# Causal attention and a cosine MLP in one kernel: GpSimd's copy of q and k moved ahead of the halves of x

## The chip, the cores and the metric

The kernel runs on one core of one Trainium2 chip. The metric is the device time of one execution in microseconds. Times of the trace are counted from the start of its span. PE is the matrix engine, PEld its weight load, DVE is VectorE, ACT is ScalarE, POOL is GpSimd, and SP issues most of the DMAs.

## The reference

```python
# q, k, v: 4 batches, 12 heads, 448 positions, 64 per head, float32
scores = scale * q @ k^T                      # causal: masked above the diagonal
attn   = softmax(scores)
x      = (attn @ v) as [4*448, 12*64]         # 1792 x 768
h      = x @ w_in                             # 768 x 2048
out    = (h * cos(h)) @ w_out                 # 2048 x 768
```

All is float32. The kernel keeps that precision in the matrix products of the second part by splitting a number into a high half and a low half and multiplying three pairs of halves.

## The kernel before

The schedule is written out by hand: each engine takes its instructions in the order in which the program lists them, and an instruction that must wait holds up all that stand behind it on its engine or queue.

Attention is a loop over 24 pairs of heads (steps i = 0 to 23). Each step works on several pairs at once: the scores, masks and exponentials of pair i; the product of the probabilities with v, and the division, of pair i-2; the transposes of the probabilities of pair i-1; and the transposes of q and k of pair i+2.

- q and k of a pair are loaded by SP into one of two buffers `raw` (`load_raw`, L260; one buffer lies in the tile `land`, the other is the tile `raw`). GpSimd copies them into one of two buffers `nat`, which both lie in `land`, with the two heads side by side (`interleave`, L267). PE transposes `nat` (`transpose_in`, L336), and the result is evacuated to `flat` (`evac_in`, L340 and L342). Pairs 0 and 1 are loaded straight into `nat`.
- The scores (L383) go to PSUM, and DVE adds the mask and takes the row's minimum in one instruction for each of seven parts (`masked`, L392). ACT takes the exponentials (`exps`, L399).
- The probabilities are transposed on PE (`tp`, L416) and evacuated to `pm` by DVE (L340) and ACT (L342). `av` multiplies them with v (L436), and DVE divides (`divide`, L464 to L466).
- `put_out` transposes the quotient on PE (L475), ACT copies it to `xf` (L494), and GpSimd makes the high half and the low half of x from it (`finish_hi`, L499 and L500), which go to `xa` and `xb`. In some steps x is cut between these two and the halves are four instructions.
- Beside this, the weights of the first groups are converted: SP loads a piece into `st` every second step (L117, L122), DVE works on it (L139 and L142 in one step, L148 and L152 in the next), and GpSimd does the rest (L145, or L156 and L157), which the program keeps in the list `postponed` and lists at the start of the next step (`take_postponed`).

Before the change a step begins on GpSimd's queue with the copy of pair i+2, then the postponed weight work, and near the step's end come the halves of x of pair i-2. On SP's queue a step begins with the load of pair i+3, then v of pair i. In steps 0, 1 and 2 the order is written out on its own.

After attention the second part follows, in which PE works on large products; the loads of its weights go through the tile `land` as well, once attention has done with it.

Of the kernel before, what the change touches and what calls it, by code (L numbers as in the profile page):

```python
# [21 lines left out]
def kernel(  # L22
# [205 lines left out]
    def attention(filler_of, postponed):  # L228
        with (
# [15 lines left out]
            N = len(pairs)  # L245
# [7 lines left out]
            def half(h):  # L253
                return slice(h * R, (h + 1) * R)

            def load_raw(i):
                b, hp = pairs[i]
                raw[i] = raw_t[i % 2]
                for h, src in ((1, k), (0, q)):
                    nc.sync.dma_start(  # L260
                        out=raw[i][half(h)],
                        in_=src[b, 2 * hp : 2 * hp + 2].rearrange("j (p c) d -> p j (c d)", c=NM),
                    )

            def interleave(i):
                nat[i] = nat_t[:, i % 2]
                nc.gpsimd.tensor_copy(  # L267
                    nat[i].rearrange("p c (j d) -> p c j d", j=2),
                    raw.pop(i).rearrange("p j (c d) -> p c j d", c=NM),
                )  # L270
# [60 lines left out]
            def transpose_in(i, bs, order=None):  # L331
                for h in range(2):
                    qkt[i, h] = flat[:, 2 * h + i % 2, 0:S], banks8[:, bs[h], 0:S]
                for c, h in order or [(c, h) for c in range(NM) for h in range(2)]:
                    o = qkt[i, h][1].rearrange("p (r c) -> p c r", c=NM)
                    nc.tensor.transpose(o[:, c], nat[i][half(h), c], ident[half(h), half(h)])  # L336
# [7 lines left out]
            def evac_in(i, h, dve=False):  # L344
                evac(*qkt[i, h], dve)
# [11 lines left out]
            def col(m):  # L357
                return slice(COL[m], COL[m] + 1)

            def open_step(i):  # L360
                prob[i] = prob_t[i % 3]
                stats[i] = at.tile([P, 8], F32, tag="stat", bufs=3, name="stat")
# [4 lines left out]
            def place(i, m):  # L367
                b, o = spot(i, m)
                return banks8[:, b, o * R : (o + m) * R]

            def probs(i, m):
                return prob[i][:, AT[m] * R : (AT[m] + m) * R]
# [16 lines left out]
            def masked(i, *ms):  # L389
                for m in ms:  # L390
                    z = W if m == TURNED else S - m * R
                    nc.vector.tensor_tensor_reduce(  # L392
                        out=probs(i, m), in0=place(i, m), in1=mask[:, z : z + m * R], scale=-scale,
                        scalar=3.0e38, op0=ALU.add, op1=ALU.min, accum_out=stats[i][:, col(m)],
                    )

            def exps(i, *ms):
                for m in ms:
                    nc.scalar.activation(  # L399
                        probs(i, m), probs(i, m), AF.Exp, scale=-1.0, bias=stats[i][:, col(m)]  # L400
                    )
# [66 lines left out]
            def turn_out(i):  # L468
                t = outs[i].rearrange("p b n d -> p b (n d)")
                for x in range(4):  # L470
                    for h, ms in enumerate((ROW[1::2], ROW[::2])):
                        if x < len(ms):
                            b, n, _ = PLACE[ms[x]]
                            c = (T0, 4 * R)[h] + x * R
                            nc.tensor.transpose(  # L475
                                banks8[:, obank(i) + 1 - h, c : c + R],
                                t[half(h), b, n * P : (n + 1) * P], ident[half(h), half(h)],
                            )
# [9 lines left out]
            def finish(i):  # L488
                xf = at.tile([P, S], F32, tag="xf", bufs=2, name="xf")
                x = xf.rearrange("p (n r) -> p n r", r=R)  # L490
                ob = obank(i)
                for e, (b, c) in ((1, (1, T0)), (0, (0, 4 * R))):
                    o = banks8[:, ob + b, c : c + (4 - e) * R]
                    nc.scalar.copy(x[:, e::2], o.rearrange("p (n r) -> p n r", r=R))  # L494
                return xf

            def finish_hi(i, xf):
                for hi, lo, cs in x_of(i):
                    nc.gpsimd.tensor_copy(hi, xf[:, cs])  # L499
                    nc.gpsimd.tensor_tensor(lo, xf[:, cs], f32(hi), op=ALU.subtract)  # L500
# [3 lines left out]
            def fill(n):  # L504
                if not extra:
                    spare = itertools.cycle((7, 6))
                    extra.append(filler_of(lambda: banks8[:, next(spare)]))
                for _ in zip(range(n), extra[0]):
                    pass
# [7 lines left out]
            def put_out(i):  # L517
                turn_out(i)
                finish_hi(i, finish(i))

            def take_postponed():
                while postponed:
                    postponed.pop(0)()
# [7 lines left out]
            interleave(2)  # L531
            load_v(0)
            for i in range(N):
                if 2 < i + 2 < N:
                    interleave(i + 2)
                take_postponed()
                if i + 3 < N:
                    load_raw(i + 3)
                if i:
                    load_v(i)  # L540
                open_step(i)
                if i < 3:
                    scores(i, slice(0, 4))
                    if i < 2:
                        transpose_in(i + 1, TB_)
                    else:
                        tp(0, 1, (0, 1))
                    scores(i, slice(4, 8))
                if i == 0:
                    masked(i, 4, 3)  # L550
                    exps(i, 4)
                    evac_in(1, 0, True)
                    evac_in(1, 1)
                    masked(i, 7, 6, 5, 1, 2)
                    exps(i, 3, 7, 6, 5, 1, 2)
                    yield i
                    continue
                if i == 1:
                    masked(i, 4, 3, 7)
                    evac_in(2, 0)  # L560
                    evac_in(2, 1)
                    exps(i, 4, 3)
                    open_ptr(0)
                    tp(0, 0, (0, 1))
                    evac_out(0, 0, (0, 1), 0)
                    masked(i, 6, 5, 1, 2)
                    exps(i, 7, 6)
                    yield i
                    continue
                if i == 2:  # L570
                    transpose_in(3, TB_)
                    evac_out(0, 1, (0, 1), 0)
                    exps(1, 5, 1, 2)
                    masked(i, 4, 3)
                    exps(i, 4, 3)
                    masked(i, 7, 6)
                    exps(i, 7)
                    evac_in(3, 0, True)
                    evac_in(3, 1)
                    masked(i, 5, 1, 2)  # L580
                    exps(i, 6, 5, 1, 2)
                    av(0)
                    divide(0)
                    transpose_in(4, TB_)
                else:
                    scores(i)
                    if i < N - 1:
                        evac_in(i + 1, 0)
                        evac_in(i + 1, 1)
                    masked(i, 4, 3, 7, 6, 5, 1, 2)  # L590
                    exps(i, 4, 3, 7, 6, 5, 1, 2)
                    av(i - 2)
                    divide(i - 2)
                    if i < N - 2:
                        transpose_in(i + 2, TB_)
                G1, G2 = ((7, 4), (5, 6)) if i < N - 1 else (TB_, (4, 5))
                open_ptr(i - 1)
                tp(i - 1, 0, G1)
                evac_out(i - 1, 0, G1, 0)
                tp(i - 1, 1, G2)  # L600
                evac_tp(i - 1, 1, G2, 1)
                evac_tp(i - 1, 1, G2, 0, i % 2 == 0)
                if i == N - 1:
                    fill(4)
                put_out(i - 2)
                if i == N - 1:
                    fill(2)
                    open_ptr(i)
                    tp(i, 1, (4, 5))
                    evac_out(i, 1, (4, 5), 0)  # L610
                    tp(i, 0, TB_)
                    evac_out(i, 0, TB_, 0)
                yield i
# [785 lines left out]
    with tc.manual_schedule():  # L1399
        def filler_of(get):  # L1400
            return m1(ring, 0, *order_a[0], early, get)
# [75 lines left out]
```

## Time and profile before

| | |
|---|---|
| median of 3 runs | 600.83 us |
| lowest and highest run | 599.5 and 601.18 us |
| time of the profiled execution | 601.19 us |
| its span | 599.4 us |
| PE busy | 581.5 us, 97% |
| PE weight loads busy | 538.8 us, 90% |
| DVE busy | 455.2 us, 76% |
| POOL busy | 417.7 us, 70% |
| ACT busy | 402.2 us, 67% |

The shares are averages over the whole span. The attention loop and the second part have different limits, so a change in one of them is read from the rows of that part. The span is shorter than the time of the execution by 1.8 us.

### The profile page before, as it was taken

Reading aid. Unit: us, or ns where it says so; the run is one execution under the profiler, and the core shown is the slowest. Engines: PE = TensorE matmul, PEld = TensorE weight load, DVE = VectorE, ACT = ScalarE, POOL = GpSimd, SP = SyncE. Lnnn points to the kernel's source line nnn. Section 1 sums busy time; section 2 is a strip of 40 time slices with the busy share of each in tenths; the row PEclk is TensorE's granted clock in tenths of the full one; section 3 lists DMA queues with packets and bytes.
Section 4 is the critical chain, followed back from the end, with each engine's and each line's share of the span. In section 5 each row is a group of like instructions: output and inputs, shape, how many; then the busy total and the mean of one; then the engine's idle time right before and its main releaser. Section 6 shows DMA issues by size and latency. Waiting matters only on the chain.

```text
span 599.4 us, 15299 instructions
## 1 busy us (share of the span) xinstructions
PE 581.5 (97%) x5895; PEld 538.8 (90%) x5895; DVE 455.2 (76%) x952; ACT 402.2 (67%) x788; POOL 417.7 (70%) x448
## 2 busy tenths in 40 slices
PE   8999998899999999999999999999999999999996
PEld 6788887788899998899999999999999999999996
DVE  4889888887586787787777777853487887887786
ACT  5999998888667786877777778731544653654540
POOL 1466565654559786878778887744579878878894
PEclk9999999999999999999999999999999999999998
DMA  9958778565058868787969788499988547648105
GB/s 171 202 142 187 174 178 196 129 167 160 10 189 273 329 194 323 240 309 241 348 196 335 249 270 322 173 338 390 394 294 308 209 149 275 220 170 297 52 1 158
DMA packets 92601, 134.30 MB, mean 224 GB/s; under 512 B 35024, under 2 KB 76864, under 8 KB 92528
## 3 DMA queue, kind: packets, MB, share of 16 engines
q1 hardware_dynamic: 84832, 106.91, 57.8%
q0 software_dynamic: 4928, 24.78, 11.3%
q10 hardware_dynamic: 2768, 1.64, 1.0%
q8 instruction: 46, 0.75, 0.5%
q14 instruction: 27, 0.22, 0.1%
HBM read 83.36 MB, written 49.94 MB: 222 GB/s over the span
## 4 chain that ended last, share of the span: by engine, by line
PE 73%; POOL 6%; ACT 6%; DVE 5%; DMA 5%; issue 3%; SPq 0%; ACTq 0%; POOLq 0%; DVEq 0%
PE banks L733 18%; PE banks L1162 13%; PE banks L1182 13%; PE banks L638 6%; PE banks L637 6%; PE banks L639 6%; POOL land L267 3%; ACT pm L342 2%; PE banks L336 2%; PE banks L1199 2%; PE banks L416 2%; PE banks L1086 2%; PE banks L436 2%; DMA vn<-in_v_dram 2%; DMA land<-in_moe_w_in_dram 2%
## 5 line engine op out<-in xcount | busy, mean ns | idle before, releaser
L721 DVE TENSOR_TENSOR acc<-acc,banks 128x768 f32<-128x768 f32 (+1 forms) x122 | 112.6, 932 | 42.3 <-PE banks L733 32.1
L733 PE MATMUL banks<-w,gh 128*128 128x384 f32 x512 | 109.9, 335 | 1.2 <-DVE acc L721 1.2
L733 PEld LDWEIGHTS banks<-w,gh 128*128 128x128 f32 x512 | 90.7, 188 | 3.0 <-DVE acc L721 1.8
L638 PE MATMUL banks<-xa,w 128*128 128x512 f32 x192 | 75.2, 392 | 0.0
L639 PE MATMUL banks<-xa,w 128*128 128x512 f32 x192 | 75.0, 391 | 0.0
L637 PE MATMUL banks<-xa,w 128*128 128x512 f32 x192 | 74.9, 390 | 0.0
L399 ACT ACTIVATE pb<-pb,stat 128x256 f32<-128x256 f32 (+6 forms) x168 | 71.1, 527 | 3.3 <-DVE stat L392 3.3
L392 DVE CUSTOM_DVE_ANT_0 pb<-banks,mask 128x256 f32<-128x256 f32 (+6 forms) x168 | 59.9, 420 | 9.5 <-PE banks L383 9.4
L733 PE MATMUL banks<-w,gl 128*128 128x384 f32 x256 | 65.1, 335 | 0.0
L757 POOL TENSOR_TENSOR w<-ct,w 128x768 fp32r<-128x768 f32 x28 | 51.9, 1852 | 17.4 <-ACT w L756 12.8
L645 ACT ACTIVATE ni<-banks 128x512 int32<-128x512 f32 (+1 forms) x64 | 34.4, 538 | 33.5 <-PE banks L639 19.9
L647 DVE SCALAR_TENSOR_TENSOR r<-ni,banks 128x512 f32<-128x512 int32 (+1 forms) x56 | 35.0, 626 | 23.5 <-ACT ni L645 23.0
L664 POOL TENSOR_TENSOR gl<-r,gh 128x512 fp32r<-128x512 f32 x32 | 41.5, 1299 | 15.9 <-ACT gh L663 15.6
L436 PE MATMUL banks<-vn,pm 128*64 128x65 f32 (+1 forms) x1344 | 48.5, 223 | 0.0
L649 ACT ACTIVATE r<-r 128x512 f32<-128x512 f32 (+1 forms) x56 | 32.8, 586 | 22.2 <-DVE r L647 21.7
L733 PEld LDWEIGHTS banks<-w,gl 128*128 128x128 f32 x256 | 46.4, 188 | 0.0
L383 PE MATMUL banks<-flat 64*64 64x64 f32 (+5 forms) x768 | 44.5, 358 | 1.6 <-DVE stat L392 0.5
L436 PEld LDWEIGHTS banks<-vn,pm 128*64 128x64 f32 (+1 forms) x1344 | 44.3, 137 | 1.9
L652 DVE SCALAR_TENSOR_TENSOR r<-r,banks 128x512 f32<-128x512 f32 (+1 forms) x56 | 35.0, 626 | 14.1 <-ACT r L650 14.1
L1162 PE MATMUL banks<-xb,bb 128*128 128x384 f32 x234 | 44.7, 334 | 0.0
L383 PEld LDWEIGHTS banks<-flat 64*64 64x64 f32 x768 | 32.9, 132 | 11.9 <-DVE pm L340 3.2
L639 PEld LDWEIGHTS banks<-xa,w 128*128 128x128 f32 x192 | 36.0, 188 | 7.5
(143 smaller groups left out, 1429.7 us busy)
## 6 DMA issues: line engine op xcount, KB each, us to landing
bb<-w_in_d SPq DMA_DIRECT2D x48, 384.0 KB, 5.5
land<-in_moe_w_in_dram SPq DMA_DIRECT2D x14, 768.0 KB, 6.1
land<-in_moe_w_out_dram SPq DMA_DIRECT2D x14, 768.0 KB, 5.7
w_out_d<-w POOLq DMA_DIRECT2D x14, 768.0 KB, 6.3
big<-w_out_d SPq DMA_DIRECT2D x25, 384.0 KB, 4.6
w_in_d<-w POOLq DMA_DIRECT2D x7, 768.0 KB, 4.3
raw_d<-ct POOLq DMA_DIRECT2D x14, 384.0 KB, 7.8
vn<-in_v_dram SPq DMA_DIRECT2D x48, 96.0 KB, 4.1
```

What stands on the lines that cost most here:

```text
L383: nc.tensor.matmul(place(i, m)[heads(j ^ SWAP[m]), c : c + z - a], lhsT=qt[heads(j), (m - 1) * R : m * R], rhs=kt[heads(j), a:z], start=ba ...
L392: nc.vector.tensor_tensor_reduce(out=probs(i, m), in0=place(i, m), in1=mask[:, z : z + m * R], scale=-scale, scalar=3.0e38, op0=ALU.add, o ...
L399: nc.scalar.activation(probs(i, m), probs(i, m), AF.Exp, scale=-1.0, bias=stats[i][:, col(m)])
L436: nc.tensor.matmul(banks8[half(h), ob + b, c : c + E1], lhsT=lhsT, rhs=rhs, start=start, stop=stop)
L637: yield nc.tensor.matmul(hv, lhsT=wh[:, f], rhs=x[:, 0, cc, t], start=(cc == 0), stop=False)
L638: yield nc.tensor.matmul(hv, lhsT=wh[:, f], rhs=x[:, 1, cc, t], start=False, stop=False)
L639: yield nc.tensor.matmul(hv, lhsT=wl[:, f], rhs=x[:, 0, cc, t], start=False, stop=(cc == NCC - 1))
L721: nc.vector.tensor_tensor(d, d, o, op=ALU.subtract)
L733: nc.tensor.matmul(o[:, e, 0:EH], lhsT=a[:, cs], rhs=w[:, e * EH : (e + 1) * EH], start=(x == 0), stop=(x == 5),)
L757: nc.gpsimd.tensor_tensor(w[:, 1], tf, f32(w[:, 0]), op=ALU.subtract)
L1162: nc.tensor.matmul(o, lhsT=w[:, u, k * P : (k + 1) * P], rhs=x[k][:, v], start=k + m == 0, stop=k == K - 1 and m == 2,)
L1182: nc.tensor.matmul(o[:, b % 2, 0:EH], lhsT=g_ops[i][u][:, c * P : (c + 1) * P], rhs=wouts[g, i][:, v], start=(x == 0), stop=(x == 2),)
```

## The change

The copy of q and k (`interleave`) leaves the start of the step. From step 2 on it is listed near the step's end, just ahead of `put_out`, and it is for pair i+3 instead of i+2. In steps 0 and 1, which are written out on their own, it is the last line before `yield`, for pairs 3 and 4. The loads of q and k are listed one step earlier: step 0 loads pairs 3 and 4, and each further step loads pair i+4. A buffer of `raw` is still free for its load when the copy of the pair two before it is done. In step 1, masks 6 and 5 are listed together with masks 4, 3 and 7, ahead of the evacuation of the first transposes of the probabilities. No instruction is added or removed.

```diff
             for i in range(N):
-                if 2 < i + 2 < N:
-                    interleave(i + 2)
                 take_postponed()
-                if i + 3 < N:
-                    load_raw(i + 3)
+                if i == 0:
+                    load_raw(3)
+                if i + 4 < N:
+                    load_raw(i + 4)
                 if i:
                     load_v(i)
                 open_step(i)
...
                     exps(i, 3, 7, 6, 5, 1, 2)
+                    interleave(3)
                     yield i
                     continue
                 if i == 1:
-                    masked(i, 4, 3, 7)
+                    masked(i, 4, 3, 7, 6, 5)
                     evac_in(2, 0)
                     evac_in(2, 1)
                     exps(i, 4, 3)
                     open_ptr(0)
                     tp(0, 0, (0, 1))
                     evac_out(0, 0, (0, 1), 0)
-                    masked(i, 6, 5, 1, 2)
+                    masked(i, 1, 2)
                     exps(i, 7, 6)
+                    interleave(4)
                     yield i
                     continue
...
                 if i == N - 1:
                     fill(4)
+                if i + 3 < N:
+                    interleave(i + 3)
                 put_out(i - 2)
```

## Rows read from the trace of the kernel before

**Rows 1.** Busy time by stretch: from:to, length, then PE, PEld, DVE, ACT, POOL

```profile
90.00:130.00 40.00, 35.54 (x965) 31.48 (x963) 34.00 (x136) 35.33 (x90) 24.39 (x42) 1.00 0.70 172
...
183.00:238.00 55.00, 53.84 (x275) 49.02 (x275) 42.33 (x52) 41.69 (x64) 43.69 (x42) 1.00 0.80 285
238.00:582.00 344.00, 344.00 (x1869) 329.13 (x1869) 255.73 (x355) 204.72 (x363) 265.54 (x257) 1.00 0.73 253
```

**Rows 2.** Chain of waits, one steady step: start, length, what

```profile
42.06 0.88 POOL land L267
...
42.98 0.65 PE banks L336 x14
...
45.73 0.64 POOL xa L499
```

**Rows 3.** Waits from 24 to 134 us: total, times, longest

```profile
PE banks L336 <- POOL land L267: 8.2, 18, 0.9
...
DVE pm L340 <- PE banks L416: 5.5, 12, 0.7
```

**Rows 4.** Timeline of POOL: start, length, instruction, in brackets idle before and releaser

```profile
43.35 0.73 POOL L157 TENSOR_TENSOR w<-ct,w 128x256 fp32r<-128x256 f32 x1
...
51.69 0.56 POOL L499 CAST xa<-xf 128x448 fp32r<-128x448 f32 x1 [2.66 <-ACT xf L494]
```

**Rows 5.** Timeline of DVE: divisions and pm copies of the loop

```profile
26.89 0.61 DVE L340 COPY pm<-banks 128x448 f32<-128x448 f32 x1
...
38.21 0.62 DVE L340 COPY pm<-banks 128x448 f32<-128x448 f32 x1
...
42.63 0.17 DVE L464 TENSOR_SCALAR r<-banks 128x8 f32<-128x8 f32 x1 [0.17 <-PE banks L436]
...
44.11 1.16 DVE L340 COPY pm<-banks 128x448 f32<-128x448 f32 x2 [0.34 <-PE banks L416]
...
48.45 0.17 DVE L464 TENSOR_SCALAR r<-banks 128x8 f32<-128x8 f32 x1
...
49.64 0.62 DVE L340 COPY pm<-banks 128x448 f32<-128x448 f32 x1
...
102.03 1.16 DVE L340 COPY pm<-banks 128x448 f32<-128x448 f32 x2 [0.73 <-PE banks L416]
...
131.99 0.62 DVE L340 COPY pm<-banks 128x448 f32<-128x448 f32 x1
```

**Rows 6.** Timeline of DVE: two instructions of the weight conversion

```profile
45.52 0.43 DVE L142 SCALAR_TENSOR_TENSOR ct<-st,ct 128x256 uint32<-128x256 uint32 x1
...
50.18 0.42 DVE L148 SCALAR_TENSOR_TENSOR ct<-st,ct 128x256 uint32<-128x256 uint32 x1
```

**Rows 7.** Timeline of SP's queue, step 1 and the start of step 2

```profile
13.24 1.12 SPq L286 DMA_DIRECT2D vn<-in_v_dram  x2
14.41 0.49 SPq L117 DMA_DIRECT2D st<-in_moe_w_in_dram  x1
15.69 0.60 SPq L260 DMA_DIRECT2D raw<-in_k_dram  x1
```

**Rows 8.** Timeline of DVE: step 1's pm copy and mask 6, step 3's conversion and first mask

```profile
13.94 0.62 DVE L340 COPY pm<-banks 128x448 f32<-128x448 f32 x1 [1.05 <-PE banks L416]
14.48 0.55 DVE L392 CUSTOM_DVE_ANT_0 pb<-banks,mask 128x384 f32<-128x384 f32 x1
...
21.60 0.28 DVE L139 TENSOR_SCALAR ct<-st 128x256 uint32<-128x256 uint32 x1
...
23.26 0.42 DVE L392 CUSTOM_DVE_ANT_0 pb<-banks,mask 128x256 f32<-128x256 f32 x1 [0.91 <-PE banks L383]
```

**Rows 9.** DMA issues from 0 to 40 us: KB each, median us to landing

```profile
vn<-in_v_dram SPq DMA_DIRECT2D x14, 96.0 KB, 4.7
```

**Rows 10.** Landing times of the loads into the tile raw

```profile
DMA to landing us min/median/max: 3.3/4.2/6.7
```

**Rows 11.** Landing times of the loads of weight pieces into st, 0 to 40 us

```profile
DMA to landing us min/median/max: 3.6/4.5/6.0
```

## The prediction

> **What bounds the kernel now.** I first read the busy time by stretch. From 238 to 582 us PE works without a gap, 344.00 of 344.00 us; in attention it does not, 35.54 of 40.00 us between 90 and 130 [rows 1]. A change inside attention can only win what PE waits there, and what it wins passes on nearly whole, because everything after it is PE's own work.
>
> Next I read the chain of waits for one steady step. It is a ring: GpSimd's copy into land (42.06), the PE transposes that read it (42.98), ScalarE's copies of what they give, then GpSimd's halves of x (the first at 45.73), and behind the second the next copy into land [rows 2]. GpSimd takes its work in program order: halves of x(i-3), copy i+2, postponed weight work, halves of x(i-2). So the copy that PE needs in the middle of step i stands behind halves that need the end of step i-1. The ring sets the pitch of the loop.
>
> The list of waits over 24 to 134 us gives the price: PE's matmuls waited 8.2 us in 18 times for land, and VectorE's evacuation of the transposes (pm) waited 5.5 us in 12 times for PE [rows 3]. GpSimd itself has time: it stood idle 2.66 us before a half of x [rows 4].
>
> **The change part by part.**
>
> *The copy ahead of the halves.* Nothing is added or removed in steady state: the same copies, the same loads. Copy i+3 now runs in step i, after the postponed work of step i. In step 6 of the old trace the halves end about 42.0, the copy takes 0.88 us, and the postponed pair behind it ends at 43.35 + 0.73 = 44.08 [rows 2, 4]. With the copy behind it, the pair ends near 43.2 and the copy near 44.1. It is wanted by the transposes of step 7, a pitch after 42.98, near 48.5. The wait of PE for land goes, with some 4 us in hand. The halves need ScalarE's x only near 45.7, so they don't slip.
>
> What is late next? VectorE. I follow it from one pm copy to the next. Even to odd step: 44.11 to 49.64, 5.53 us, with no wait for PE ahead of the second pm: the division starts at 48.45 and pm follows 1.19 us on [rows 5]. Odd to even: pm at 38.21, division at 42.63, pm at 44.11; the last leg is 1.48 us because pm waited for PE's transposes. With PE earlier it would be 1.19, so the leg is 4.42 + 1.19 = 5.61 us. The last pm of the stretch lies at 131.99 and the first at 26.89: 105.10 us for 18 legs. In the steps where x is cut in two, the waits are longer (0.73 us at 102.03), and all of it is the ring [rows 5]. New: 9 x 5.53 + 9 x 5.61 = 100.26 us. The gain is 105.10 - 100.26 = 4.84 us.
>
> Bounds of this term: the odd division waits 0.17 us for PE, whose scores may start a little earlier once ScalarE's copies do; if every leg is 5.53, the gain is 5.56 us. PE's own waits would allow 8.2 us at most, if VectorE gave way too [rows 3, 5]. I take 4.84, because the scores of a step wait for VectorE's pm copy, and VectorE's legs of 5.53 us show no wait for PE ahead of their end. Below: nothing, if the copy came late again; that is a rival.
>
> *The loads a further step ahead.* raw(i+4) is issued in step i and still waits for copy i+2 of the same buffer, now in step i-1. From copy d-2 to copy d there are two steps, some 11.1 us. Landing takes 3.3 to 6.7 us, median 4.2 [rows 10], the pair of issues about 1.3 us (two of 0.60 and what lies between [rows 7]) and the copy 0.88, so 2.2 to 4.8 us are left. On SP's queue v, a weight piece and, in some steps, a store or more v stand behind the waiting load and wait with it; v takes 1.12 us to issue and a piece 0.49 [rows 7], so SP has caught up within the step. Cost: nothing. The cover is gone at a landing above some 9 us.
>
> *The start.* Here the order on SP changes for real. Before: the load of step 1 waited for the first copy only, so v(1) was issued at 13.24, the first weight piece at 14.41, and the next load at 15.69, behind copy 3 [rows 7]. After, the load in front of v(1) is the one that waits for copy 3, which can't come sooner because its data land then. So v(1) moves from 13.24 to about 17.0 and the piece from 14.41 to about 18.2, 3.8 us each. They take 4.7 and 4.5 us (median) to land in this stretch [rows 9, 11]: v(1) at 22.2 for its second half, the piece near 22.7. Step 3's product with v(1) and its first mask come at about 23.3; VectorE waited 0.91 us before that mask [rows 8], and the weight conversion stands just ahead of it on VectorE, from 21.6 to 22.4. A piece that lands at 22.5 costs nothing; at 22.7 it costs 0.2 us; after 6.0 us of landing, the longest [rows 11], near 24.2, it costs 1.7 us. I take 0.2. The loads that went out between are fewer, so the landing may also be faster.
>
> *The two masks.* In step 1, masks 6 and 5 (0.55 us and a little less) go ahead of a pm copy for which VectorE idled 1.05 us [rows 8]. Their scores are done only about when that idle time ends, so at worst the pm copy is 0.4 us later, at best the last masks of the step are 0.5 us sooner, and the scores of step 2 with them. ScalarE works back to back there. Taken: 0.2 us won, between +0.4 and -0.5.
>
> *A port.* Starting its copy elsewhere, GpSimd meets other VectorE work. In the trace a half of x that starts during VectorE's weight conversion (45.52 to 45.95) takes 0.64 us, one that starts under masks takes 0.56 [rows 2, 4, 6]: a loss of 0.08 us on GpSimd, which has idle time. The new copies of steps 6 and 7 start near 43 and 48, and the nearest conversions are at 45.52 and 50.18, more than a microsecond off. Cost: nothing. The Trainium skill, "SBUF — State Buffer", section "Who interferes with whom", speaks against the change here: a VectorE instruction with two SBUF inputs and a GpSimd instruction that reads SBUF contend, and the second to start stands still for the whole of the first. By that rule a conversion caught behind a copy would lose up to the copy's length; the 0.08 us above is the only trace of it in the rows, smaller than a full block. By the rule the sum changes only if copy and conversion meet, which is the fourth rival.
>
> **Sum.** -4.84 in the loop, +0.2 at the start, -0.2 for the masks: -4.8 us. The profiled execution took 601.19 us (span 599.4 and 1.8 around it), so 596.4 us; the median of the runs, 600.83, lies 0.36 below it, which gives 596.0.
>
> **The rivals.**
>
> 1. *The start slips.* The piece or v(1) lands late and VectorE holds everything behind it. For: 3.8 us later on the queue, and landings up to 6 us or more in a busy stretch. Against: less traffic ahead of it. With 1.7 us lost: 597.7; with something more from the masks, up to 599.
> 2. *More comes back than VectorE's legs show.* If VectorE's small gaps also close, all 8.2 us of PE: 600.83 - 8.2 = 592.6; halfway, 594.3. Against: even legs hold no such gap.
> 3. *No change.* The copy stands earlier in the order, but its data don't. Copy d waits for raw(d), issued only when SP gets past v, stores and weight pieces; if that and the landing take 10 us, PE waits as before, and the halves of x are now behind the late copy. Nor would it help if another ring had the same pitch. For: SP's queue is in order and often waits. Against: the margin of 2.2 to 4.8 us above, and legs of 5.53 us that already exist. Time: 600.8.
> 4. *Slower: copy and conversion collide.* If copy i+3 is late by more than about 1 us, it runs into VectorE's conversions, whose operands lie in SBUF (0.42 us for the one at 50.18). VectorE would be the new bound, so each stop goes straight into the leg. With half a copy (0.44 us) in each of 18 steps it is +7.9, less 4.8: +3.1, or 603.9. It decides from 4.8/18 = 0.27 us a step. Against: 0.08 us is all that a meeting cost so far, and the copy is early. This is what the full block of the Trainium skill's "SBUF — State Buffer" ("Who interferes with whom") would do here; no row of this case shows one.
>
> **How the numbers follow.** Forecast (594.8 to 597.4) 0.62; rival 1 0.14; rival 2 0.11; rival 3 0.07; rival 4 0.06. The time is that of the likeliest, 596.0. The range reaches down through half of rival 2 and up through nearly all of rival 1: 593.5 to 599.0. Faster or slower by over 0.3% is 1.8 us, about what a measurement of this kernel can tell from no change: the first three cases are faster, nearly always, 0.86; within it 0.08; slower 0.06.
>
> **What would show it.** Right: no PE wait for land after step 3; copies into land end some 4 us before their transposes; pm to pm of 5.5 to 5.6 us in every leg, also where x is cut; the pm copies right behind the divisions; attention's last pm near 127; the rest the same, shifted. The start's term is right if the first conversion begins by 21.8 or so. Wrong: a GpSimd wait for raw in the loop (rival 3), conversions of over 0.5 us or a gap ahead of them in the loop (rival 4), a VectorE gap before the first conversion of over 1 us (rival 1), legs under 5.4 us (rival 2). The bubble of PE between 183 and 238 us (53.84 us busy of 55.00 [rows 1]) may move by a microsecond either way; the range holds that.

## The result and the profile after

| | before | after |
|---|---|---|
| median of 5 runs | 600.59 us | 594.49 us |
| lowest and highest | 599.5 to 601.18 | 593.66 to 597.18 |
| profiled execution, its span | 601.19, 599.4 | 593.66, 591.9 |
| ratio after to before | | 0.9907, 95% interval 0.988 to 0.9934 |

The change makes the kernel 0.93% faster, 6.1 us in the medians. The profiled execution of after is the fastest of its five, that of before the slowest of its five, so their spans differ by more, 7.5 us. A second set of runs of the changed kernel gave 595.67 us against 600.59, ratio 0.9922 (0.9909 to 0.9936).

The list of waits of the changed kernel, 24 to 130 us (total, times, longest), answers to [rows 3]:

```profile
PEld banks L383 <- DVE pm L340: 3.6, 18, 0.2
DVE pb L392 <- PE banks L383: 3.3, 11, 0.6
...
ACT pm L342 <- PE banks L416: 1.5, 9, 0.2
```

PE's wait for land (8.2 us) and VectorE's wait of pm for PE (5.5 us) are both gone from the loop. What is left goes the other way: PE's weight loads wait 0.2 us a step for VectorE's pm copy, as they did before (3.0 us in 19 times).

The timeline of GpSimd after shows why, and answers to [rows 4]:

```profile
36.55 0.61 POOL L145 TENSOR_TENSOR st<-st 128x256 f32<-128x256 f32 x1
37.11 0.93 POOL L267 COPY land<-land 128x896 f32<-128x896 f32 x1
40.44 0.56 POOL L499 CAST xa<-xf 128x448 fp32r<-128x448 f32 x1 [2.40 <-ACT xf L494]
```

The copy ends at 38.04. PE's timeline has the transposes that read it without any wait at 42.64:

```profile
42.64 0.65 PE L336 MATMUL banks<-ident,land 64*128 64x64 f32 x14
```

The copy stands 4.6 us in hand where it had nothing, and the halves of x still find GpSimd waiting for them.

VectorE's timeline after, divisions and pm copies, answers to [rows 5] (the last is step 21, as 131.99 there):

```profile
27.76 0.61 DVE L340 COPY pm<-banks 128x448 f32<-128x448 f32 x1
...
38.50 0.61 DVE L340 COPY pm<-banks 128x448 f32<-128x448 f32 x1
...
42.83 0.17 DVE L464 TENSOR_SCALAR r<-banks 128x8 f32<-128x8 f32 x1
...
43.87 1.14 DVE L340 COPY pm<-banks 128x448 f32<-128x448 f32 x2
48.20 0.17 DVE L464 TENSOR_SCALAR r<-banks 128x8 f32<-128x8 f32 x1
49.24 0.61 DVE L340 COPY pm<-banks 128x448 f32<-128x448 f32 x1
...
103.75 0.61 DVE L340 COPY pm<-banks 128x448 f32<-128x448 f32 x1
...
109.12 1.14 DVE L340 COPY pm<-banks 128x448 f32<-128x448 f32 x2
...
125.22 0.61 DVE L340 COPY pm<-banks 128x448 f32<-128x448 f32 x1
```

A leg is the time from one step's pm copy to the next step's. Legs are 5.36 to 5.42 us long (38.50 to 43.87, 43.87 to 49.24, and 103.75 to 109.12 where x is cut), but for two of 5.72 and 5.77. The 18 legs take 125.22 - 27.76 = 97.46 us, where they took 105.10 [rows 5].

The start is where time was lost. SP's queue and VectorE after, to hold against [rows 7] and [rows 8]:

```profile
15.80 0.59 SPq L260 DMA_DIRECT2D raw<-in_k_dram  x1
16.49 0.60 SPq L260 DMA_DIRECT2D raw<-in_q_dram  x1
17.14 1.87 SPq L286 DMA_DIRECT2D vn<-in_v_dram  x2
19.05 0.49 SPq L117 DMA_DIRECT2D st<-in_moe_w_in_dram  x1
```

```profile
19.96 1.15 DVE L340 COPY pm<-banks 128x448 f32<-128x448 f32 x2
23.64 0.29 DVE L139 TENSOR_SCALAR ct<-st 128x256 uint32<-128x256 uint32 x1 [2.52 <-DMA st<-in_moe_w_in_dram]
...
24.31 0.42 DVE L392 CUSTOM_DVE_ANT_0 pb<-banks,mask 128x256 f32<-128x256 f32 x1
```

The first weight piece is issued at 19.05 instead of 14.41, VectorE stands still 2.52 us for it, and step 3's first mask comes at 24.31 instead of 23.26.

The ledger of the two traces, counted on VectorE's pm copies: step 3's is 0.87 us later (27.76 against 26.89), step 21's is 6.77 us earlier, so the loop gave 7.64 us. From there to the end 0.7 us more came. The busy time by stretch after (behind each stretch its length, then PE's busy time) shows that PE's one bubble in the second part shrank by about as much, from 1.16 [rows 1] to 0.34 us. That this belongs to the change is not shown: in the twelve profiles of this case the stretch from step 21's pm copy to the end takes 466.7 to 469.0 us, with 467.4 before.

```profile
90.00:125.00 35.00, 34.60 (x970) 31.21 (x964) 32.73 (x138) 34.54 (x89) 24.28 (x41) 1.00 0.78 188
...
177.00:232.00 55.00, 54.66 (x281) 49.84 (x280) 43.23 (x54) 42.50 (x66) 44.12 (x42) 1.00 0.82 286
232.00:574.00 342.00, 342.00 (x1858) 327.13 (x1857) 254.20 (x353) 203.06 (x361) 264.21 (x255) 1.00 0.73 253
```

The same view for an odd and an even leg:

```profile
38.50:43.87 5.37, 5.30 (x151) 4.76 (x149) 4.84 (x21) 5.37 (x14) 3.27 (x5) 1.00 0.85 161
43.87:49.24 5.37, 5.30 (x151) 4.76 (x149) 5.18 (x22) 5.21 (x15) 3.66 (x5) 1.00 0.82 178
```

PE is now busy for 5.30 of 5.37 us by the profile's reckoning, so next to nothing of PE's idle time is left to win.

### The profile page after: what moved, and what is told of

It reads as the page before. It is cut to its first block, busy times and chain, and to the rows that moved or that the text cites. A ratio compares the mean times of both kernels' runs of the same rounds, so it can differ in the third digit from the quotient of the medians.

```text
span 591.9 us, 15297 instructions
## 1 busy us (share of the span) xinstructions
PE 581.5 (98%) x5895; PEld 539.7 (91%) x5895; DVE 453.6 (77%) x952; ACT 401.7 (68%) x788; POOL 418.2 (71%) x448
## 4 chain that ended last, share of the span: by engine, by line
PE 76%; DVE 15%; ACT 3%; DMA 2%; issue 2%; POOL 1%; SPq 0%; DVEq 0%; ACTq 0%; POOLq 0%
PE banks L737 18%; PE banks L1166 13%; PE banks L1186 13%; PE banks L642 6%; PE banks L641 6%; PE banks L643 6%; DVE pb L392 6%; PE banks L383 4%; PE banks L436 3%; DVE pm L340 2%; PE banks L1203 2%; PE banks L1090 2%; DVE on L466 2%; DMA raw_d<-ct 2%; PE banks L416 1%
## 5 line engine op out<-in xcount | busy, mean ns | idle before, releaser
L643 PEld LDWEIGHTS banks<-xa,w 128*128 128x128 f32 x192 | 36.0, 188 | 7.5
L641 PEld LDWEIGHTS banks<-xa,w 128*128 128x128 f32 x192 | 36.1, 188 | 7.3
```

The lines of the kernel that those rows point to most:

```text
L641: yield nc.tensor.matmul(hv, lhsT=wh[:, f], rhs=x[:, 0, cc, t], start=(cc == 0), stop=False)
L643: yield nc.tensor.matmul(hv, lhsT=wl[:, f], rhs=x[:, 0, cc, t], start=False, stop=(cc == NCC - 1))
```

## The experiments

The theory: the place of the copy behind the halves of x closed a ring that set the pitch, and its new place opens it; the loads' earlier issue is not needed and costs at the start. The rivals: the loads are what matters; the masks are; the start is swallowed by slack in the loop.

**The masks alone**, on the kernel before:

```diff
-                    masked(i, 4, 3, 7)
+                    masked(i, 4, 3, 7, 6, 5)
...
-                    masked(i, 6, 5, 1, 2)
+                    masked(i, 1, 2)
```

> The kernel before with the two masks of step 1 moved forward and nothing else. Theory A (the masks free step 2's scores): the division of step 2 starts near 18.9 us instead of 19.49, the loop keeps its legs of 5.5 to 6.3 us from pm copy to pm copy and its 8.2 us of PE's waits for land, and the time is 0.5 us below before, 600.1. Rival B (ScalarE works back to back there and hides them): the division stays at 19.5 and the time at 600.6.

Measured: 601.44 us against 600.83, ratio 1.0004 (0.9991 to 1.0016): no difference that can be told. The loop stays as it was, 25.20 to 130.23, 105.03 us, with 8.1 us of PE's waits for land. In the trace the masks seem to win a little: from the first mask of the kernel to step 2's pm copy it takes 19.57 - 7.77 = 11.80 us, and 20.54 - 8.17 = 12.37 us in the kernel before; in the changed kernel it is 12.06. Over all the profiles with the masks moved it is 11.75 to 12.35 us, so the gain is 0.0 to 0.6 us, under what the runs resolve. Neither theory of the expectation is refuted by the times; the trace is nearer to A.

**The copy behind the halves**, loads and masks as changed:

```diff
-                if i + 3 < N:
-                    interleave(i + 3)
                 put_out(i - 2)
+                if i + 3 < N:
+                    interleave(i + 3)
```

> The changed kernel with the copy listed right behind the halves of x of the same step instead of ahead of them; loads and masks as changed. Theory A (the ring of copy, transposes, ScalarE's copies and halves sets the pitch): the ring is back, PE waits about 8 us for land over some 18 steps, legs of 5.5 to 6.3 us, and the late start of the first weight piece stays: about 601. Rival B (the gain comes from the earlier loads): legs of 5.4 us and 594.5.

Measured: 604.82 us, ratio 1.0056 (1.0035 to 1.0076): slower than before. Its waits, 20 to 137 us:

```profile
PEld banks L336 <- POOL land L267: 10.9, 19, 1.0
...
PE banks L336 <- POOL land L267: 8.3, 19, 0.9
DVE pm L340 <- PE banks L416: 5.4, 12, 0.7
...
DVE ct L139 <- DMA st<-in_moe_w_in_dram: 1.6, 1, 1.6
```

One line listed one place later brings back the whole ring: 8.3 us of waits and 18 legs of 104.92 us together. The earlier loads alone give nothing in the loop and leave the late piece at the start. The rival that the loads are the source falls. The profile is 4.0 us longer than that of the kernel before; 1.8 us of it lie between step 2's pm copy and step 3's (8.15 us instead of 6.35), and the rest in the time of the first mask and behind the loop, where the profiles of all kernels differ.

**The copy without the earlier loads**, masks as changed:

```diff
-                if i == 0:
-                    load_raw(3)
-                if i + 4 < N:
-                    load_raw(i + 4)
+                if i + 3 < N:
+                    load_raw(i + 3)
```

> The changed kernel with the loads of q and k listed where they were before (pair i+3 in step i), so only the copy and the masks have moved. Theory A (the place of the copy is what counts, and it has some 4 us in hand): no PE wait for land in the loop, legs of about 5.4 us as in the changed kernel, and since v and the first weight piece of step 1 no longer stand behind the load that waits for copy 3, VectorE's wait of 2.52 us for that piece is gone: 1.0 to 1.6 us below the changed kernel, about 593.2. Rival B (the loads must run a further step ahead): the copies wait for raw in every step, PE waits for land again, legs of 5.6 us or more, 597 or later.

Measured: 594.09 us, ratio 0.9891 (0.9866 to 0.9917). No wait of PE for land in the loop, 17 of the 18 legs within a few hundredths of 5.37 or at it, one of 5.91, 97.22 us in all. The piece is issued at 15.41 and VectorE does not wait for it. One copy, at 28.24, waited 2.6 us for its load and ran into a conversion, which took 0.96 us instead of 0.43; that leg is still 5.38 us. So the loads' step ahead buys nothing that the legs show: the copy's 4 us in hand cover a load listed a step later. The time is not the 593.2 that was expected; the interval holds both that and the changed kernel's time.

**The start reordered**: pair 5 is loaded at the start of step 2 instead of step 1, all else as changed.

```diff
-                if i + 4 < N:
+                if i == 2:
+                    load_raw(5)
+                if i != 1 and i + 4 < N:
                     load_raw(i + 4)
```

> The changed kernel with the load of pair 5 listed at the start of step 2 instead of step 1, ahead of that of pair 6; all else as changed. Theory A (VectorE's wait for the first weight piece lies on the path): v and the piece of step 1 are issued near 13.2 and 14.5 us, the first conversion starts near 21 instead of 23.64, step 3's first mask near 22.7 instead of 24.31, everything after it is earlier by as much: 1.0 to 1.6 us below the changed kernel, about 593.2. Rival B (the loop has slack that swallows the start): the same time as the changed kernel, 594.5.

Measured: 592.38 us, ratio 0.9864 (0.9846 to 0.9883). VectorE's timeline has the first conversion without a wait:

```profile
20.74 0.28 DVE L139 TENSOR_SCALAR ct<-st 128x256 uint32<-128x256 uint32 x1
```

It and the changed kernel were then timed again, side by side.

> The changed kernel as it is, beside the reordered start on one chip. Every theory expects 594.5 within a few tenths; the first conversion waits about 2.5 us for its piece again if that wait belongs to the order on SP's queue, and not if it was one bad landing.

> The changed kernel with pair 5 loaded at the start of step 2, beside the changed kernel. Theory A (the first piece's wait is on the path): 1.5 to 2.5 us below the changed kernel of the same call, 592.4. Rival B (the two differ by chance of the runs): within 0.6 us of it.

Measured: 593.95 (ratio 0.9887, 0.9864 to 0.9910) against 595.67 us for the changed kernel. The differences are 1.7 us here and 2.1 us between the two first sets; the intervals just touch. In the traces, step 2's pm copy to step 3's takes 7.80 and 7.20 us in the two profiles of the changed kernel, 5.92 and 5.52 with the start reordered. The 5.92 holds a collision of its own (below), so against the clean 5.52 the late piece costs 2.3 and 1.7 us there, and the loop does not swallow it.

The wait that was expected again, of about 2.5 us, was 0.97 us in the second profile. The piece itself was no earlier for VectorE: issued at 18.21, it took 5.5 us to land, and the conversion began at 23.69, against 23.64 in the first profile. VectorE came later, as the first mask of the kernel did (at 9.57 us, not 7.90). The rest of that leg's loss is a collision: L142, late by then, met GpSimd's work on a half of x and took 1.32 us instead of 0.43:

```profile
24.07 1.32 DVE L142 SCALAR_TENSOR_TENSOR ct<-st,ct 128x256 uint32<-128x256 uint32 x1
```

```profile
23.98 1.14 POOL L500 TENSOR_TENSOR xa<-xf,xa 128x448 fp32r<-128x448 f32 x1
```

So the lateness belongs to the order on SP's queue; in one profile it shows as a wait alone, in the other as a wait and a collision.

**What sets the pitch now.** In the reordered start the third evacuation of the transposes is put always on VectorE, or always on ScalarE; in the kernel it changes with the step.

```diff
-                evac_tp(i - 1, 1, G2, 0, i % 2 == 0)
+                evac_tp(i - 1, 1, G2, 0, True)     # evac_dve; evac_act: no True
```

> The reordered start, and in odd steps the third evacuation of the transposes on VectorE instead of ScalarE, as in even steps. Theory A (with the ring gone, the pitch of 5.37 us is VectorE's chain pm, scores, masks, division): an odd step's masks start 0.3 to 0.35 us later because two pm copies and the conversion no longer fit ahead of them, odd legs of 5.7 us, even legs 5.37, the time about 3 us up at 595. Rival B (ScalarE is the bound): ScalarE loses 0.44 us in odd steps, legs of 5.37 us or less, no loss.

> The reordered start, and in even steps too the third evacuation of the transposes on ScalarE: VectorE has 0.54 us less work in an even step, ScalarE 0.44 us more. Theory A (the pitch of 5.37 us is the chain pm, PE's scores, masks, division, in which VectorE waits for the scores anyway when it has only one pm copy): even legs stay at 5.37. Rival B (ScalarE is the bound): even legs of 5.4 to 5.8 us. Rival C (VectorE's sheer work is the bound): even legs shorter than 5.3 us.

Measured, one run each: 597.66 and 594.11 us; so the legs say more here than the times.

With all on VectorE, six of the ten odd legs are 5.60 to 5.72 us (38.18 to 43.89 is one), one is 6.34, and three are 5.38 to 5.44; even ones are mostly 5.37, while ScalarE, relieved, waits for VectorE. The legs came as expected but not by the expected sum. In the odd legs of 5.71 a conversion takes 0.76 us instead of 0.43: 0.33 us of it is a collision (below). Two odd legs without one, from 72.33 and from 116.11, are 5.38, though VectorE has 0.54 us more to do in them (a third, 5.62, holds a short stop of PE):

```profile
116.11 1.16 DVE L340 COPY pm<-banks 128x448 f32<-128x448 f32 x2
...
120.24 0.29 DVE L392 CUSTOM_DVE_ANT_0 pb<-banks,mask 128x128 f32<-128x128 f32 x1
...
120.45 0.16 DVE L464 TENSOR_SCALAR r<-banks 128x8 f32<-128x8 f32 x1
...
121.49 1.15 DVE L340 COPY pm<-banks 128x448 f32<-128x448 f32 x2
```

Its masks start 0.19 us later than in the changed kernel (1.93 us behind pm instead of 1.74), and the division makes up for it. It follows the last mask after 0.21 us. In the changed kernel it follows after 0.38 us (42.45 to 42.83):

```profile
42.45 0.29 DVE L392 CUSTOM_DVE_ANT_0 pb<-banks,mask 128x128 f32<-128x128 f32 x1
```

So there the division waits some 0.17 us for something else than the masks. It reads PE's product with v, which ends at 42.70 in PE's timeline and at 48.07 in the next step, 0.13 us before each division.

With all on ScalarE, nearly every leg is 5.43 us and ScalarE works back to back, as its timeline shows, while VectorE waits 0.47 us for the scores ahead of even masks. These even legs lie in the range of rival B: with 0.44 us more, ScalarE has become the bound.

```profile
43.39 1.47 ACT L342 COPY pm<-banks 128x448 f32<-128x448 f32 x3
44.67 0.69 ACT L494 COPY xf<-banks 128x192 f32<-128x192 f32 x2
45.14 1.09 ACT L342 COPY flat<-banks 128x448 f32<-128x448 f32 x2
45.99 3.02 ACT L399 ACTIVATE pb<-pb,stat 128x256 f32<-128x256 f32 x7
48.82 1.47 ACT L342 COPY pm<-banks 128x448 f32<-128x448 f32 x3
```

This run can't settle rival C by itself, because ScalarE's 5.43 us would hide a shorter leg. The clean legs of evac_dve settle it: VectorE's sheer work is not the bound, since 0.54 us more of it lengthens nothing. ScalarE's is not either: in an even leg of evac_dve (77.71 to 83.08) ScalarE is busy 5.21 us, VectorE 5.18 and PE 5.30, and the leg stays at 5.37. So theory A is right that a chain through pm and the division sets the pitch, but the masks are not in it. It runs over pm, PE's scores and its product with v, the division, and pm again, and PE is busy in it but for 0.07 us a leg. ScalarE's work lies within 0.06 us of the same length.

**GpSimd held busy**: in the reordered start, each copy from pair 6 on is done three times into the same place.

```diff
-                nc.gpsimd.tensor_copy(
-                    nat[i].rearrange("p c (j d) -> p c j d", j=2),
-                    raw.pop(i).rearrange("p j (c d) -> p c j d", c=NM),
-                )
+                src = raw.pop(i)
+                for _ in range(3 if i > 5 else 1):
+                    nc.gpsimd.tensor_copy(
+                        nat[i].rearrange("p c (j d) -> p c j d", j=2),
+                        src.rearrange("p j (c d) -> p c j d", c=NM),
+                    )
```

> The changed kernel with each copy from pair 6 on done three times into the same place, so GpSimd is busy 1.86 us longer a step and the copies run on into VectorE's weight conversions. Theory A (GpSimd has slack and at most 0.1 us passes between the engines): the extra copies cost nothing or little, legs of 5.4 us, 594.5 to 596. Rival B (a VectorE conversion stands still while a GpSimd copy runs): conversions of 0.8 to 1.3 us instead of 0.28 and 0.43, legs 0.5 to 0.9 us longer in most steps, 603 to 610.

Measured: 601.94 us, ratio 1.0014 (0.9996 to 1.0032). All that the change and the reordered start won is lost. Two lines of the conversion, with shortest, median and longest in ns:

```profile
L142 DVE SCALAR_TENSOR_TENSOR ct<-st,ct x12: 427/1086/1194, 21.1 to 147.9; 128x256 uint32<-128x256 uint32 x12
```

```profile
L152 DVE SCALAR_TENSOR_TENSOR ct<-st,ct x12: 424/965/1190, 26.8 to 150.4; 128x256 f32<-128x256 f32 x12
```

Legs alternate between 5.95 and 5.44 us, longer still where x is cut. Theory A of this expectation falls; B's conversions came, its longer legs only in every second step, where the conversion has no idle time of VectorE to hide in, and its time was too high.

**The start without a collision**: the reordered start, and in step 2 the copy of pair 5 behind the halves.

```diff
-                if i + 3 < N:
+                if 2 < i < N - 3:
                     interleave(i + 3)
                 put_out(i - 2)
+                if i == 2:
+                    interleave(5)
```

> The reordered start, and in step 2 alone the copy of pair 5 behind the halves of x, so that it can't run during the first weight conversion. Theory A (a conversion stands still while a copy runs, seen once at 1.18 us instead of 0.43 in the reordered start): first conversions of 0.28 and 0.43 us, 5.5 to 5.6 us from step 2's pm copy to step 3's, the copy still in time for its transposes, and the time 592 to 594, at most 0.4 us from the reordered start. Rival B (the late copy is late for its transposes): a wait of PE for land in step 3 and 594 or more.

Measured: 592.52 us, ratio 0.9876 (0.9854 to 0.9898). The first conversions take 0.28 and 0.43 us and the leg is 5.62, as expected. Of rival B there is a trace: PE's weight loads waited 0.3 us for land once, and the next leg is 5.47 us. The time can't be told from that of the reordered start (592.38 and 593.95), so what this collision costs in all is not shown. Both are faster than the kernel before. The reordered start was 2.1 and 1.7 us faster than the changed kernel; this one was not timed beside it.

## Why the prediction was right, and where not

The time, 594.49, lies in the range (593.5 to 599.0) and on the side that was forecast, 1.5 us under the 596.0 and 0.3 us below the likeliest case's own bounds. Two terms were mis-sized, and their errors partly cancel: in the profile the loop gave 2.8 us more than was taken, and the start cost some 1.3 us more. By the prediction's own signs rival 2 (legs under 5.4 us) and rival 1 (a gap of over 1 us ahead of the first conversion) both came, and pulled opposite ways. That the time lies within the range is in part luck. That it lies on the forecast side, and by the forecast cause, is not.

- *The ring and its end: right.* The copy comes 4.6 us early (some 4 were foretold), no PE wait for land is left, the halves don't slip, and the copy one place later brings it all back (copy_behind).
- *What comes next: taken to be VectorE, and the term too small.* The step that failed is "Even to odd step: 44.11 to 49.64, 5.53 us, with no wait for PE ahead of the second pm". There was one. In the same trace PE's transposes of q and k begin at 48.52, and pm follows 1.12 us later, just as it does after 42.98 at 44.11 in the step where the wait was listed:

```profile
48.52 0.65 PE L336 MATMUL banks<-ident,land 64*128 64x64 f32 x14 [0.19 <-POOL land L267]
```

Free of PE, pm follows the division after 1.04 us (48.20 to 49.24), not 1.19. VectorE's wait of 0.15 us lay in every "free" leg and in no list of its own. A sign of it stood in [rows 3]: PE waited for land 18 times, once a step, and VectorE for PE only 12 times. The odd leg lost 0.44 us between division and pm, and 0.08 us more between its first mask and the division (2.67 us before, 2.59 after), so all legs are 5.37: 7.64 us instead of 4.84, and 8.28 in the second profile of the changed kernel. This is what rival 2 said; its price of 8.2 us was nearly right for the loop. The prediction let VectorE's legs set the new pitch, and the runs show PE there, busy 5.30 us of 5.37 (evac_dve and the rows of the two legs).
- *The start: right in kind, too small.* +0.2 us was taken and 1.7 named as the bad end. From step 2's pm copy to step 3's the changed kernel takes 1.45 and 0.85 us more than the kernel before (7.80 and 7.20 against 6.35), and 2.3 and 1.7 us more than the clean 5.52 with the start reordered. In the first profile the piece went out at 19.05 and not at 18.2, because v's two issues ahead of it took 1.87 us instead of 1.12, and it landed 4.6 us later. In the second it went out at 18.21, as forecast, and landed 5.5 us later. Both give about 23.65, a microsecond behind the 22.7 of the prediction, and VectorE came to the conversion at 21.1 and 22.7. start_order takes the cost away without touching the loop, so this is shown.
- *The masks: right, as far as can be told.* 0.2 us was taken; the traces give 0.0 to 0.6.
- *The loads: right that they cost nothing in the loop.* They buy nothing there either (copy_only).
- *The port: the price was wrong, the place right.* "0.08 us is all that a meeting cost so far" came from a half of x that met a conversion. A conversion that meets a copy stands for most of it (0.75 us of 0.93 in start_order). In the loop of the changed kernel none does (its conversions take 0.43 us at most), so rival 4 did not come, but it was nearer than it looked: 2 us more of GpSimd's work per step spend the whole gain (copy_thrice).
- *No change*, rival 3, did not come: no copy waits for its load in the steady loop.

## What to carry to other kernels

When an in-order engine takes a job that is due next behind one that only the end of this step releases, the two close a ring, and putting the due job first opens it. The gain ends at the next bound, here PE's own busy time, so set that beside the legs first. To size such a gain, look for the wait in every leg by its distance from the suspected releaser; a list of waits leaves short ones out. Loads moved ahead on one queue also hold back what stands behind them, so check the start, where there is no slack.

## What the hardware showed

*A GpSimd copy stops a VectorE conversion.* The timelines of VectorE and GpSimd in the start of copy_only:

```profile
22.56 0.66 DVE L139 TENSOR_SCALAR ct<-st 128x256 uint32<-128x256 uint32 x1
23.26 0.83 DVE L142 SCALAR_TENSOR_TENSOR ct<-st,ct 128x256 uint32<-128x256 uint32 x1
```

```profile
22.15 0.93 POOL L267 COPY land<-raw 128x896 f32<-128x896 f32 x1 [3.83 <-PE banks L475]
23.25 0.56 POOL L499 CAST xa<-xf 128x448 fp32r<-128x448 f32 x1 [0.17 <-ACT xf L494]
```

L139 takes 0.28 us alone and ends here 0.14 us behind the copy. L142 starts 0.01 us behind GpSimd's cast and takes 0.83 us instead of 0.43. In the reordered start one L142, 0.03 us behind a copy, took 1.18, and in the second profile of the changed kernel one took 1.32. Each of these three ends 0.27 to 0.28 us behind GpSimd's instruction. The Trainium skill, "SBUF — State Buffer", section "Who interferes with whom", says that of a VectorE instruction with two SBUF inputs and a GpSimd instruction that reads SBUF, the second to start stands for the whole of the first. L142 is such a one, and these runs agree nearly: it lost 0.40 us to a cast of 0.56, and 0.75 us to a copy of 0.93. L139 has one input; it was stopped too, and why is not shown. The 0.08 us of the prediction seemed to speak against the rule. There the conversion was first, and GpSimd's cast had only its last part to wait for.

*PE stops for nothing the profile shows.* The two long legs of the changed kernel and three in start_order_again (6.51, 6.51 and 5.72 us) hold stops of PE or of its weight loads such as this one of the latter:

```profile
70.67 0.77 PE L416 MATMUL banks<-ident,pb 64*128 64x64 f32 x18 [0.69 <-issue]
```

They come between 60 and 76 us in some executions, once near 47 us (copy_only), and cost 0.75 us in one profile, 2.6 in another and none in the second profile of the changed kernel. The first mask of the kernel, too, comes anywhere from 7.8 to 9.6 us, and the stretch behind the loop takes 466.7 to 469.0 us. The runs of one kernel spread over 3 us and more; that these three make up the spread is likely and not shown. Their cause wasn't tried and stays open.
